# A block-sparse attention and gated Fourier convolution kernel: the forward transform of the last four pairs by two and then by three, the frequencies in another order, and a priority of its own for every operation

## The chip, the cores and the metric

The kernel runs on one core of a Trainium2 chip. The metric is the device time of one execution in microseconds (us). The kernel before was run three times: 232.38, 234.02 and 234.77 us, median 234.02 us.

## The reference

The inputs are q, k and v of shape (4 batches, 8 heads, 768 positions, 64 dimensions) and three matrices for the second half. For each head the 768 positions are cut into 12 blocks of 64. A query attends causally to its own block and to the three blocks whose mean key has the highest product with it:

```python
k_rep = k.reshape(B, H, n_blocks, block, D).mean(axis=3)
gate_scores = np.einsum('bhsd,bhnd->bhsn', q, k_rep)
...
top_idx = np.argsort(gate_scores, axis=-1)[..., -top_k:]
...
attn = softmax(q k^T / 8 where the mask allows) @ v
```

The attention output x, with heads side by side (768 x 512 for each batch), goes through a gated long convolution, which is circular over the 768 positions:

```python
proj = x @ w_proj                      # 512 -> 3 * 512: x1, x2, x3
X2 = np.fft.rfft(x2, n=S, axis=1)
H = np.fft.rfft(filter_fft, n=S, axis=0)[None, :, :]
x2_conv = np.fft.irfft(X2 * H, n=S, axis=1)
y = x1 * x2_conv * x3
return y @ w_out
```

The output is (4, 768, 512) in float32.

## The kernel before, in words

**Units of work.** Two heads make a pair; there are 16 pairs (index g), four for each batch. All data is in tiles of 128 partitions, matmuls run in float16 and accumulate in PSUM, which has 8 banks. While attention lasts, two pairs of banks hold scores, and four single banks serve everything else.

**Attention of a pair.** `prep(g)` loads k and q, transposes k on TensorE (L360), sums its blocks on VectorE (L363), copies it to `kt` on ScalarE (L373), does the same for q (L424, L427, L430), computes the gate (L483), finds the third largest value (L493 to L511) and puts the block mask beside the transposed q (L528, L535). Pairs from 9 on get the transposed q by transposing DMAs (L462, L466). `attn(g)` makes, for each of two heads, three pieces of scores (L558), the exponential on ScalarE (`ex`, L565), a causal cut of the diagonal on GpSimd (`sel`, L570), the product with v (`pv`, L588), and the division by the row sum on VectorE (L597, L601), which gives the tile `xn`. So there are 96 pieces of scores and 96 exponentials.

**The forward transform of a pair.** `xn` has 6 chunks of 128 positions. `eo` (L626, VectorE or GpSimd) adds and subtracts the two halves of the sequence: even frequencies need only the sum, odd ones only the difference, each of 3 chunks. `st1` then multiplies these chunks with a table `F` of cosines and sines: in part 0, three matmuls of 256 columns (L638) and six of 128 columns (L645), in part 1 three of 256 columns (L638). `XT` (L651, VectorE or ScalarE) evicts the result. A transposing DMA (L620) gives `xT`, the attention output with its 128 columns on partitions.

**The convolution of a batch.** `hyena(b)` needs all four pairs of its batch: `s2` projects the spectrum (L747), `t` multiplies it with the filter's spectrum `HA`, `HB`, `HA0` (L756, VectorE), `Y` combines the products (L766), `x13` computes the two gates x1 and x3 (L783), evicted as `x1` (L789) and `prod` (L792), `cv` goes back to positions (L810), `ce`, `sd`, `yT` (L819, L825, L831) finish the product, `op` is the output projection (L841), `osb` its eviction (L845) and a DMA (L848) stores it. The filter's spectrum is made once at the start: `hf` (L697, L702) and `ha` (L707, ScalarE).

**What sets the order.** Nothing in the kernel waits by hand. `build` lists all operations with what they read and write, a cost for each engine that may take them, and a due time `vt`. `plan` is a list scheduler: again and again it takes, on the engine that can start first, the ready operation of smallest due time, gives it buffers and, where several engines may run it, picks the one that would end it first (with a bias `d_<tag>` against VectorE). The instructions are then emitted in that order, each engine runs its own in order, and the compiler adds the semaphores. A due time is a formula in the pair's or batch's number with some 50 constants in `PAR`, and one offset `v_<tag>` shared by all operations of a kind:

```python
vt += self.par.get("v_" + tag, 0.0)
```

Until a planned time (`warm_until`) holes on TensorE are filled with matmuls whose results nobody reads (`filler`, L945, 128x256); there are 116. All loads and stores are issued by one queue, SyncE's. The semaphores of the DMAs are eight, used in turn, and a DMA waits for the one eight places ahead of it.

**What the change touches.** `PAR` and `Graph.add`; `e_phase`, `e_iota`, `e_nyq` (L178 to L198), which fill the row of frequencies `colv` that `F` is made from; the pool `eo` (three tiles of 128x384); `eo`, `st1` in `attn` (L555 to L656); `e_ha`, `e_h0` in `filt` (L706 to L721), and `e_t` in `hyena` (L753).

Of the kernel before, what the change touches and what calls it, by code (L numbers as in the profile page):

```python
# [16 lines left out]
P = 128  # L17
# [10 lines left out]
TR = ("T1", "T2", "xT")  # L28
QS = 128.0
# [15 lines left out]
for _pi, _segs in enumerate(PIECES):  # L45
    for (_col, _kc, _q0, _w) in _segs:
        for _c in range(_q0 // P, (_q0 + _w) // P):
# [4 lines left out]
    direct=2, tm=9, kin=16, p0=-2.69, p1=0.365, pvlag=-6.582, dlag=1.76, dlen=1.383, h0=4.856,  # L52
    hlen=3.36, f0=-1.155, f1=7.084, ld=-3.238, s2a=-2.037, s2b=1.216, x0=0.354, x1=1.108, c0=-1.101,
    c1=2.132, o0=1.271, ahead=46.953, delta=0.033, queue=5.995, w0=1.489, wl=1.839, wlag=-9.917, warm_until=32.306,
    tr0=-18.919, trl=6.39, fill0=0.877, v_yT=7.627, v_sd=-1.517, d_k2=6.956, v_trig=-4.154, v_ldq=1.131, v_max=-5.158,
    v_g=0.972, v_Y=0.635, v_k2=0.499, v_rec=-6.814, v_small=-3.021, v_gate=0.152, v_km=0.106, d_x1=3.233, d_shQ=2.566,
    v_xT=-0.742, v_prod=-3.06, v_ldv=0.502, d_yT=8.721, v_ks=0.515, v_osb=-10.289, v_ldk=0.513, v_kT=0.073, v_gT=-1.053,
    d_md=-0.495, d_trig=6.615, v_qT=0.164, v_mT=0.152, v_lt=-2.205, v_fe=7.674, d_eo=-0.025, v_md=-2.102, v_phase=2.124,
    v_shQ=5.115, v_ldf=0.27, d_Y=3.198, v_sel=-7.798, v_warm0=4.967, v_x1=-4.181, v_ldw=0.046, v_tab=0.848, v_va=5.426,
    v_iota=-3.776, d_XT=-0.933, v_qh=0.379, v_h0=4.716, v_eblk=9.913, v_id32=-1.815, v_st=2.29, v_nyq=-4.563, v_s2=-2.561,  # L60
    v_st1=-0.047, v_XT=-3.549, v_t=-1.696, v_ql=-0.667, v_hf=-3.271, d_g=2.878, d_ce=12.21, d_osb=6.098, d_fill=0.038,
    v_w=-6.92, v_ce=0.546, v_fill=7.615, v_op=0.842, v_pv=-3.144, d_w=0.456, v_nrm=4.319, v_ha=-6.505, v_id16=4.506,
    v_eo=3.749, v_x13=-0.318, d_fe=-2.864, v_cv=-2.842, v_sc=0.099, v_T2=-3.366, v_T1=-1.079, d_qh=1.789, v_pq=-5.732,
    d_pq=12.199, v_ex=0.491, v_nid=0.437, a0=0.0, o1=1.0, pen_dve=0.205, late=2.0,
)

POOLS = dict(kn=2, qn=3, vn=2, k2=1, qx=4, ks=2, km=3, m8=2, gs=2, nm=1,
             kt=4, qt=4, va=4, ex=8, rec=2, xn=2, eo=3, XT=7, xT=8, t=8, Y=1, x1=3,
# [15 lines left out]
class Op:  # L84
    __slots__ = ("i", "eng", "emit", "deps", "bufs", "alloc", "vt", "lock", "size", "tag",
                 "start", "done", "on", "pre", "nd", "succ", "ready", "quad")


class Graph:
    def __init__(self, par):  # L90
        self.ops, self.par = [], par

    def add(self, tag, vt, eng, emit, rd=(), wr=(), res=(), lock=False, size=0, quad=0):
        o = Op()
        vt += self.par.get("v_" + tag, 0.0)
        o.i, o.tag, o.vt, o.eng, o.emit, o.lock, o.size = len(self.ops), tag, vt, eng, emit, lock, size
        o.quad = quad
        deps = set()

        def norm(xs):  # L100
            return [x if isinstance(x, tuple) else (x, 0) for x in xs]

        bufs = []
        for b, p in norm(rd):
            deps.update(b.w.get(p, ()))
            b.r.setdefault(p, []).append(o)
            bufs.append(b)
        for b, p in norm(wr):
            deps.update(x for x in b.w.get(p, ()))
            deps.update(x for x in b.r.get(p, ()) if x is not o)  # L110
            b.w.setdefault(p, []).append(o)
            bufs.append(b)
        deps.discard(o)
        o.deps = list(deps)
        o.bufs = list({id(b): b for b in bufs}.values())
        for b in o.bufs:
            b.left += 1
        o.alloc = list({id(b): b for b in o.bufs + list(res)}.values())
        self.ops.append(o)
        return o  # L120
# [21 lines left out]
def build(par):  # L142
# [35 lines left out]
    def e_phase(E, nc, en):  # L178
        ph = E.colv[32:33, :]
        nc.vector.memset(E.rowv[32:33, :], 1.0)  # L180
        nc.vector.memset(E.rowv[64:65, :], TURNS)
        nc.vector.memset(ph, 192.0)
        for x_ in cviews(ph):
            nc.vector.memset(x_[:, :, 1, :], 0.0)
        nc.vector.memset(ph[:, P:P + 1], 192.0)
# [4 lines left out]
    def e_iota(E, nc, en):  # L190
        c3, c4 = cviews(E.colv[0:1, :])
        kw = dict(channel_multiplier=0, allow_small_or_imprecise_dtypes=True)
        nc.gpsimd.iota(c3, pattern=[[1, 2], [0, 2], [2, P]], base=0, **kw)
        nc.gpsimd.iota(c4, pattern=[[1, 2], [0, 2], [2, 64]], base=256, **kw)
        nc.gpsimd.iota(E.rowv[0:1, :], pattern=[[1, HS]], base=0, **kw)

    def e_nyq(E, nc, en):
        nc.vector.memset(E.colv[0:1, P:P + 1], 384.0)  # L198
# [78 lines left out]


    kn, qn, va = {}, {}, {}
    for g in range(NG):  # L280
        b, j = divmod(g, NP)
# [22 lines left out]

    fts = []
# [238 lines left out]
    def attn(g):  # L544
        b, j = divmod(g, NP)
        xn = Buf("xn")
        E_, O_ = Buf("eo"), Buf("eo")
# [75 lines left out]
        for dst, op, f in ((E_, ALU.add, 0.0), (O_, ALU.subtract, 0.1)):  # L623
            def e_eo(E, nc, en, dst=dst, op=op):
                x_ = E.sb(xn).rearrange("p c t d -> p c (t d)")
                (nc.vector if en == "DVE" else nc.gpsimd).tensor_tensor(  # L626
                    E.sb(dst), x_[:, 0:HC, :], x_[:, HC:NQ, :], op=op)
            add("eo", v(f), {"POOL": pol(0.87), "DVE": dve(HS, 2)}, e_eo, rd=xns, wr=[dst], lock=True)
        add("xT", v(.3), {"SP": (1.25, 0)}, e_xT, rd=xns, wr=[xT[g]], size=305)
        for p_ in range(2):  # L630
            st = psb()
            lo, hi = (0, 512) if p_ == 0 else (512, S)

            def e_st(E, nc, en, p_=p_, st=st):
                o = E.bk(st)
                ev, od = E.sb(E_), E.sb(O_)
                for c in range(HC):
                    nc.tensor.matmul(o[:, 0:256], lhsT=(od if p_ else ev)[:, c, :],  # L638
                                     rhs=E.F[:, c, HS * p_:HS * p_ + 256], start=(c == 0), stop=(c == HC - 1),
                                     skip_group_check=True)  # L640
                if p_ == 0:
                    o2 = o[:, 256:512].rearrange("p (k i n) -> p i k n", k=2, i=2)
                    for i, x_ in enumerate((ev, od)):
                        for c in range(HC):
                            nc.tensor.matmul(o2[:, i], lhsT=x_[:, c, :],  # L645
                                             rhs=E.F[:, c, HS * i + 256:HS * (i + 1)]
                                             .rearrange("p (k n) -> p k n", k=2),
                                             start=(c == 0), stop=(c == HC - 1), skip_group_check=True)

            def e_XT(E, nc, en, lo=lo, hi=hi, st=st):  # L650
                (nc.vector.tensor_copy if en == "DVE" else nc.scalar.copy)(  # L651
                    E.sb(XT[g])[:, lo:hi], E.bk(st)[:, 0:hi - lo])

            add("st1", v(.5 + .25 * p_), {"PE": pe_cost([c16(256)] * 3 + ([c16(128)] * 6 if p_ == 0 else []))},
                e_st, rd=[O_] + ([E_] if p_ == 0 else []) + Fall, wr=[st], res=[XT[g]])
            add("XT", v(.55 + .25 * p_), {"ACT": act(hi - lo), "DVE": dve(hi - lo)}, e_XT, rd=[st],  # L656
                wr=[(XT[g], p_)])


    def filt():  # L660
# [27 lines left out]
        for c in range(HC):  # L688
            for kind in range(2):
# [16 lines left out]
                def e_ha(E, nc, en, c=c, kind=kind, pa=pa):  # L706
                    nc.scalar.activation((E.HB if kind else E.HA)[:, c, :], E.bk(pa), AF.Copy, bias=0.0,  # L707
                                         scale=E.crow if c == 0 else 2.0 / S)
# [4 lines left out]
                add("ha", v(.45 + .1 * (2 * c + kind)), {"ACT": act(Dm)}, e_ha, rd=[pa, cb("small")],  # L713
                    wr=[(cb("HA" if kind == 0 else "HB"), c)])

        def e_h0(E, nc, en):
            nc.vector.tensor_copy(E.HA0, E.HA[:, 0, :])
            nc.vector.tensor_copy(E.HA0[0:1, :], E.HB[0:1, 0, :])
            nc.vector.memset(E.HB[0:1, 0, :], 0.0)

        add("h0", v(1.0), {"DVE": (1.1, 1.2)}, e_h0, rd=[(cb("HA"), 0)], wr=[(cb("HB"), 0), cb("HA0")], lock=True)  # L721


    def hyena(b):
# [11 lines left out]
        for c in range(HC):  # L736
            for kind in range(2):
# [15 lines left out]
                for i, dst in enumerate((ta, tb)):  # L753
                    def e_t(E, nc, en, c=c, kind=kind, i=i, dst=dst, xa=xa):
                        m = E.HB[:, c, :] if i else (E.HA0 if kind and c == 0 else E.HA[:, c, :])
                        nc.vector.tensor_mul(E.sb(dst), E.bk(xa), m)  # L756
                    add("t", v(f, "s2a", "s2b") + .02, {"DVE": dve(Dm)}, e_t,
                        rd=[xa, (cb("HA"), c), (cb("HB"), c), cb("HA0")], wr=[dst])
# [100 lines left out]
    for g in range(NG):  # L859
        prep(g)  # L860
    for g in range(NG):
        attn(g)
    filt()
    for b in range(B):
        hyena(b)
# [6 lines left out]
def plan(par):  # L872
# [210 lines left out]
    xn=([P, NQ, 2, D], FP16), eo=([P, HC, P], FP16), XT=([P, S], FP16), xT=([P, S], FP16),  # L1083
# [17 lines left out]
def kernel(  # L1101
# [22 lines left out]
    for name, shape, dt in (  # L1124
            ("id32", [P, P], FP32), ("id16", [P, P], FP16), ("eblk", [64, S], FP16), ("colv", [P, S], FP16),
            ("rowv", [P, HS], FP16), ("warm", [P, 256], FP16), ("tab", [1, 1], FP16), ("crow", [P, 1], FP32), ("nid", [P, P], FP16), ("F", [P, HC, S], FP16),
# [39 lines left out]
```

## Time and profile before

| | |
|---|---|
| median of three runs | 234.02 us |
| the profiled execution's own time | 235.11 us |
| its span, first to last instruction | 233.4 us |
| TensorE matmuls | 223.5 us busy (96%), 2189 |
| VectorE | 184.1 us busy (79%) |
| ScalarE | 176.2 us busy (75%) |
| GpSimd | 169.3 us busy (73%) |
| DMA, 16 engines | 40.91 MB, queue 1 holds 89.9% of the span |

The span is shorter than the execution's own time by 1.7 us, which lie before the first and after the last instruction. A busy TensorE is not a full one: matmuls are pipelined, and each is shown with the time in which its results drain. What a matmul takes from the engine is the distance to the start of the next one; in unbroken rows the timeline gives 216 ns for 512 columns, 162 ns for 384, 109 ns for 256 and for a float32 transpose, 55 ns for 128, about 32 ns for the 65 columns of `pv`. This document calls that distance a slot.

### The profile page before, as it was taken

How to read it: one execution, taken by the hardware profiler on the slowest of the kernel's cores; microseconds unless marked ns; L12 is line 12 of the kernel's file. 1: busy time of each engine (PE TensorE's matmuls, PEld its weight loads, DVE VectorE, ACT ScalarE, POOL GpSimd, SP SyncE). 2: the span in 40 equal slices, each digit the busy share in tenths (PEclk: the TensorE clock that was granted, in tenths of full speed). 3: DMA queues.
4: the chain of work that ended last, by engine and by line, in shares of the span. 5: the costliest groups of instructions: out<-in, count | busy, mean ns of one | idle time of the engine just before them, and what ended most of it. 6: DMA issues, size and time to landing. Idle time of an engine off the chain costs nothing.

```text
span 233.4 us, 6222 instructions
## 1 busy us (share of the span) xinstructions
PE 223.5 (96%) x2189; PEld 151.0 (65%) x2189; DVE 184.1 (79%) x615; ACT 176.2 (75%) x295; POOL 169.3 (73%) x309
## 2 busy tenths in 40 slices
PE   7999999989898899999999999999999999999993
PEld 5787786756666577667655677676557667545551
DVE  6999779779897989998899597887986856595730
ACT  2988999999996888889957787999376675405343
POOL 8156467778669799979789999774598666069760
PEclk9999999999999999999999999999999999999999
DMA  8999999898999999999999999959912310512015
GB/s 159 330 217 201 219 194 225 174 226 203 228 213 247 216 227 176 240 223 231 187 228 204 294 186 232 178 94 163 269 61 79 70 34 3 169 46 90 3 44 225
DMA packets 120223, 40.91 MB, mean 175 GB/s; under 512 B 114304, under 2 KB 114304, under 8 KB 120192
## 3 DMA queue, kind: packets, MB, share of 16 engines
q1 hardware_dynamic: 120192, 40.51, 89.9%
q8 instruction: 17, 0.28, 0.5%
q14 instruction: 14, 0.11, 0.2%
HBM read 24.64 MB, written 6.29 MB: 133 GB/s over the span
## 4 chain that ended last, share of the span: by engine, by line
PE 70%; ACT 10%; DMA 7%; DVE 6%; issue 3%; SPq 2%; POOL 1%; DVEq 0%; ACTq 0%
PE ps L783 15%; PE ps L558 9%; PE ps L841 9%; PE ps L747 7%; PE ps L588 7%; PE ps L810 6%; DMA t<-in_moe_w_proj_dram 4%; ACT ex L565 4%; PE ps L638 4%; DMA kn<-in_k_dram 3%; PE ps L360 3%; PE ps L945 3%; ACT kt L373 3%; PE ps L645 2%; DVE ks L363 1%
## 5 line engine op out<-in xcount | busy, mean ns | idle before, releaser
L565 ACT ACTIVATE ex<-ps 128x1024 f16<-128x1024 f32 (+1 forms) x96 | 86.4, 923 | 17.5 <-PE ps L558 16.5
L570 POOL TENSOR_SCALAR_AFFINE_SELECT ex<-ex 128x256 f16<-128x256 f16 x96 | 40.1, 425 | 23.0 <-ACT ex L565 21.1
L558 PE MATMUL ps<-qt,kt 76*128 76x512 f16 (+7 forms) x256 | 50.4, 305 | 0.6 <-ACT ex L565 0.4
L783 PE MATMUL ps<-xT,wp 128*128 128x384 f16 x256 | 49.8, 326 | 0.0
L766 POOL TENSOR_TENSOR Y<-t,t 128x512 f16<-128x512 f32 (+1 forms) x32 | 40.3, 1268 | 11.3 <-DVE t L756 10.2
L373 ACT CAST kt<-ps 64x384 f16<-64x384 f32 x64 | 30.1, 472 | 6.4 <-PE ps L360 4.2
L831 POOL TENSOR_TENSOR yT<-prod,sd 128x384 f16<-128x384 f32 x32 | 32.3, 1018 | 3.6 <-DVE sd L825 2.3
L783 PEld LDWEIGHTS <-wp 128*128 128x128 f16 x256 | 24.1, 97 | 14.5 <-issue 0.3
L558 PEld LDWEIGHTS <-kt 76*128 76x128 f16 (+1 forms) x256 | 23.4, 97 | 14.6 <-issue 0.8
L588 PE MATMUL ps<-va,ex 128*128 128x65 f16 x672 | 27.2, 193 | 1.6 <-POOL ex L570 1.1
L588 PEld LDWEIGHTS <-ex 128*128 128x128 f16 x672 | 25.5, 97 | 4.8 <-POOL ex L570 1.8
L789 ACT CAST x<-ps 128x384 f16<-128x384 f32 x32 | 15.3, 478 | 14.1 <-PE ps L783 12.5
L792 DVE TENSOR_TENSOR prod<-ps,x 128x384 f32<-128x384 f32 x32 | 17.6, 552 | 8.6 <-PE ps L783 8.1
L841 PE MATMUL ps<-wo,yT 128*128 128x512 f16 x96 | 23.3, 379 | 0.0
L747 PE MATMUL ps<-wp,XT 128*128 128x512 f16 x96 | 22.5, 379 | 0.1
L651 DVE CAST XT<-ps 128x256 f16<-128x256 f32 (+1 forms) x30 | 16.1, 544 | 5.6 <-PE ps L645 3.6
L845 ACT COPY osb<-ps 128x512 f32<-128x512 f32 x24 | 14.1, 589 | 8.3 <-PE ps L841 7.9
L945 PE MATMUL ps<-warm 128*128 128x256 f16 x116 | 18.3, 293 | 1.1 <-DVE warm L1133 1.1
L363 DVE TENSOR_REDUCE ks<-ps 128x6 f32<-128x384 f32 x32 | 17.3, 548 | 2.3 <-ACT kt L373 1.3
L810 PE MATMUL ps<-G,Y 128*128 128x384 f16 x96 | 19.0, 326 | 0.0
L601 DVE TENSOR_TENSOR xn<-ps,rec 128x384 f16<-128x384 f32 x32 | 17.6, 551 | 0.7
L825 DVE TENSOR_TENSOR sd<-ce,ps 128x384 f32<-128x384 f32 x32 | 16.3, 545 | 1.6 <-ACT ce L819 1.5
(107 smaller groups left out, 376.3 us busy)
## 6 DMA issues: line engine op xcount, KB each, us to landing
kn<-in_k_dram SPq DMA_DIRECT2D x32, 192.0 KB, 4.3
vn<-in_v_dram SPq DMA_DIRECT2D x16, 384.0 KB, 5.3
qn<-in_q_dram SPq DMA_DIRECT2D x32, 192.0 KB, 4.7
out_dram<-osb SPq DMA_DIRECT2D x24, 256.0 KB, 2.3
t<-in_moe_w_proj_dram SPq DMA_DIRECT2D x12, 256.0 KB, 4.5
t<-in_moe_filter_fft_dram SPq DMA_DIRECT2D x6, 256.0 KB, 4.6
qt<-qx SPq DMA_DIRECT2D x14, 96.0 KB, 3.9
t<-in_moe_w_out_dram SPq DMA_DIRECT2D x4, 256.0 KB, 3.9
```

The source lines that it names most:

```text
L373: (nc.scalar.copy if en == "ACT" else nc.vector.tensor_copy)(E.sb(Kt[g])[r, HC * hf:HC * (hf + 1), 1 - t, :], E.bk(kp)[r, 0:HS].rearrange( ...
L558: nc.tensor.matmul(o[:, col:col + w], lhsT=E.sb(Kt[g])[0:KR[t], kc, 1 - t, :], rhs=E.sb(Qt[g])[0:KR[t], q0 // P:(q0 + w) // P, 1 - t, :], ...
L565: nc.scalar.activation(E.sb(ex)[:, 0:w], E.sp(sp)[:, 0:w], AF.Exp, scale=ESC)
L570: nc.gpsimd.affine_select(out=dv, in_=dv, compare_op=ALU.is_ge, fill=0.0, base=0, pattern=[[0, 2], [1, P]], channel_multiplier=-1)
L588: nc.tensor.matmul(o[:, 65 * c:65 * c + 65], lhsT=E.sb(exs[pi])[:, col:col + P], rhs=E.sb(va[g])[:, t, kc, :], start=(kc == 0), stop=(kc = ...
L747: nc.tensor.matmul(E.bk(xa), lhsT=w, rhs=E.wp[:, j, Dm:2 * Dm], start=(j == 0), stop=(j == NP - 1))
L766: (nc.vector if en == "DVE" else nc.gpsimd).tensor_tensor(E.sb(Y)[ro, n_, :], E.sb(x)[ri, :], E.sb(y)[ri, :], op=op)
L783: nc.tensor.matmul(E.bk(xq)[:, 0:HS], lhsT=E.wp[:, d2, 2 * Dm * m + P * dc:2 * Dm * m + P * (dc + 1)], rhs=E.sb(xT[gs[d2]])[:, cs], start= ...
L810: nc.tensor.matmul(E.bk(cv)[:, 0:HS], lhsT=E.sb(Y)[:, 3 * p_ + n_, P * dc:P * (dc + 1)], rhs=E.G[:, 3 * p_ + n_, :], start=(n_ == 0), stop ...
L831: (nc.vector if en == "DVE" else nc.gpsimd).tensor_mul(E.sb(yT)[:, dc, cs], E.sb(prod)[:, cs], E.sb(sd)[:, cs])
L841: nc.tensor.matmul(E.bk(op_), lhsT=E.sb(yT)[:, d2, P * c:P * (c + 1)], rhs=E.wo[:, d2, :], start=(d2 == 0), stop=(d2 == NP - 1))
L945: nc.tensor.matmul(E.ps[:, 3584:3840], lhsT=E.warm[:, 0:P], rhs=E.warm[:, 0:256], start=True, stop=True)
```

## The change

There are three parts.

1. For pairs 12 to 15 (`r3=12`) the forward transform splits each half once more, by three. The three chunks of the sum are combined into: the sum of all three, the first minus half of the two others, and the difference of the two others, and so for the difference of the halves. Frequencies that are multiples of three need only the first of these, one matmul in place of three; the others need two, one with `F` and one with a new table `Dt`, which is made once from `F`. The additions are done by four VectorE instructions for a pair (`r3`), and the subtraction in `eo` becomes two instructions for these pairs.
2. So that the multiples of three lie together, the frequencies are put in another order in `colv`. The constant term and the highest frequency move from the first group of columns to the third, and with them the special cases in `ha`, `h0` and `t`.
3. The due time of each of the operations comes from a table `VT` (one number for every operation, by kind and number) in place of the formula and the shared offset. The constants in `PAR` have other values too. `ha` may now run on VectorE. `eo` is one tile for both halves (two buffers in place of three single ones), `es` is new.

```diff
+    r3=12, direct=2, tm=9, kin=16, p0=-2.685, p1=0.336, pvlag=-7.813, dlag=1.811, dlen=1.366,
...
+VT = {
+    "id32": (-20.541,),
...
+    "r3": (213.925, 161.149, 176.246, 161.579,),
...
-        vt += self.par.get("v_" + tag, 0.0)
+        n = self.count[tag] = self.count.get(tag, -1) + 1
+        vt = VT[tag][n] if VT else vt
...
-        nc.gpsimd.iota(c3, pattern=[[1, 2], [0, 2], [2, P]], base=0, **kw)
-        nc.gpsimd.iota(c4, pattern=[[1, 2], [0, 2], [2, 64]], base=256, **kw)
+        for g, step in ((0, 2), (1, 4)):
+            nc.gpsimd.iota(c3[:, g], pattern=[[0, 2], [6, 64], [step, 2]], base=2 - g, **kw)
+        nc.gpsimd.iota(c4, pattern=[[3, 2], [0, 2], [6, 64]], base=0, **kw)
...
+    def e_dt(E, nc, en):
+        eng = nc.vector if en == "DVE" else nc.gpsimd
+        for i, op in enumerate((ALU.subtract, ALU.add)):
+            f1, f2 = (E.F[:, t, HS * i:HS * i + 256] for t in (1, 2))
+            eng.tensor_tensor(E.Dt[:, i], f1, f2, op=op)
+            eng.tensor_scalar_mul(E.Dt[:, i], E.Dt[:, i], 0.5 - i)
...
+                if i and r3:
+                    eng.tensor_tensor(w[:, 0:3:2], x_[:, 0:HC:2], x_[:, HC:NQ:2], op=op)
+                    eng.tensor_tensor(w[:, 1], x_[:, HC + 1], x_[:, 1], op=op)
+                else:
+                    eng.tensor_tensor(w, x_[:, 0:HC, :], x_[:, HC:NQ, :], op=op)
...
+        if r3:
+            def e_r3(E, nc, en):
+                w, s_ = E.sb(W), E.sb(es)
+                nc.vector.tensor_tensor(s_, w[:, :, 1], w[:, :, 2], op=ALU.add)
+                nc.vector.tensor_tensor(w[:, :, 1], w[:, :, 1], w[:, :, 2], op=ALU.subtract)
+                nc.vector.tensor_tensor(w[:, :, 2], w[:, :, 0], s_, op=ALU.add)
+                nc.vector.scalar_tensor_tensor(out=w[:, :, 0], in0=s_, scalar=-0.5, in1=w[:, :, 0], op0=ALU.mult,
+                                               op1=ALU.add)
+            add("r3", v(.2), {"DVE": (1.1, 1.25)}, e_r3, wr=[(W, 0), (W, 1), es], lock=True)
...
+                if r3:
+                    terms = [(w[:, p_, 0], E.F[:, 0, HS * p_:HS * p_ + 256]), (w[:, p_, 1], E.Dt[:, p_])]
+                else:
+                    terms = [(w[:, p_, c], E.F[:, c, HS * p_:HS * p_ + 256]) for c in range(HC)]
+                for n_, (l_, f_) in enumerate(terms):
+                    nc.tensor.matmul(o[:, 0:256], lhsT=l_, rhs=f_, start=(n_ == 0), stop=(n_ == len(terms) - 1), **mm)
...
+                        terms = [(2, 0)] if r3 else [(c, c) for c in range(HC)]
...
-                add("ha", v(.45 + .1 * (2 * c + kind)), {"ACT": act(Dm)}, e_ha, rd=[pa, cb("small")],
+                add("ha", v(.45 + .1 * (2 * c + kind)), {"ACT": act(Dm), "DVE": dve(Dm)}, e_ha, rd=[pa, cb("small")],
...
-            nc.vector.tensor_copy(E.HA0, E.HA[:, 0, :])
+            nc.vector.tensor_copy(E.HA0, E.HA[:, 2, :])
```

The other operations are the same as before; their places in the orders of the engines, and for some the engine, are not.

## The prediction

> **What bounds the kernel now.** I read the page first, then TensorE's timeline, then a table by stages, then the waits in the stage that had holes, then the end. The table by stages (duration; busy us and instructions of PE, PEld, DVE, ACT, POOL; clock; DMA share; GB/s):
>
> ```profile
> core 0: us, PE busy (x) PEld busy (x) DVE busy (x) ACT busy (x) POOL busy (x), PEclk, DMA share, GB/s
> 0.00:34.00 34.00, 32.69 (x306) 24.85 (x307) 28.09 (x115) 27.61 (x55) 19.43 (x44) 1.00 1.09 221
> 34.00:82.00 48.00, 43.46 (x524) 30.81 (x521) 40.46 (x158) 43.45 (x70) 36.86 (x76) 1.00 1.15 216
> 82.00:230.00 148.00, 147.37 (x1367) 95.35 (x1365) 115.59 (x344) 104.77 (x171) 113.06 (x190) 1.00 0.80 151
> 230.00:233.40 3.40, 0.00 (x0) 0.00 (x0) 0.00 (x0) 0.37 (x1) 0.00 (x0) 1.00 0.45 173
> ```
>
> Three stages are to be seen. From 82 to 230 us TensorE is full and every other engine has room: DVE 78%, ACT 71%, POOL 76%. There a slot less on TensorE is a slot less of time. To 34 us the 116 filler matmuls stand between real ones (116 x 0.109 = 12.6 us). Between, PE has holes with ACT as the fullest engine:
>
> ```profile
> 40.00:60.00 20.00, 17.99 (x238) 13.19 (x237) 15.46 (x70) 19.35 (x31) 14.84 (x33) 1.00 1.04 210
> 60.00:80.00 20.00, 17.57 (x196) 11.85 (x194) 17.82 (x62) 16.85 (x29) 16.30 (x31) 1.00 1.25 211
> ```
>
> ACT is 97% busy from 40 to 60, 84% from 60 to 80, where DVE reaches 89%. Busy time hides part of the holes, since a matmul is shown longer than its slot. Going through the starts on TensorE's timeline and taking off each slot, I find 8.6 us of holes (those over 0.06 us) from 30 to 82, 1.2 before, 0.7 from 82 to 230. The waits of PE from 30 to 82 (total, times, longest) name the larger ones:
>
> ```profile
> PE ps L588 <- POOL ex L570: 1.1, 2, 0.7
> PE ps L360 <- DMA kn<-in_k_dram: 0.9, 2, 0.7
> PE ps L528 <- DVE ks L363: 0.6, 1, 0.6
> PE ps L558 <- ACT ex L565: 0.4, 1, 0.4
> ```
>
> By start distances the `pv` holes are 0.84, 0.29, 0.56 and 0.25 us (1.9 in all: 19 of 21 products wait for one causal cut), the `kn` holes 0.44 and 0.83 (1.3). The rest, 5.4 us, is over twenty holes of 0.1 to 0.5 us. The end, from the chain of waits (start, duration):
>
> ```profile
> 198.19 0.66 PE ps L588 x21
> 198.86 2.59 PE ps L841 x12
> ...
> 224.51 5.21 PE ps L841 x24
> 229.79 0.58 ACT osb L845
> ```
>
> Twelve projections of another batch cover what the last pair needs between its last `pv` and its `st1`.
>
> **What the Trainium skill says.** "TensorE: Matmul & The Clock Gate", section "Wait — 56ns, not 53.3ns?": a warm matmul starts N/2.4 GHz + 2.5 ns after the one before. The trace agrees: 109 ns for 256 columns, 55 for 128. "Perfetto Trace Analysis", section "Identifying the Most-Contended Engine": the most contended engine can change over a kernel, and matmul busy time is a poor measure; hence the count by stages and slots. "SBUF — State Buffer", section "Who interferes with whom": a VectorE instruction with two SBUF inputs and a GpSimd one that reads SBUF block each other. `eo` and `r3` are such; the trace fits, `eo` on DVE takes 347 ns at least, 420 in the median and 917 at most.
>
> **The change part by part.** The rows used:
>
> ```profile
> L638 PE MATMUL ps<-F,eo 128*128 128x256 f16 x96 | 15.7, 272 | 0.3
> L645 PE MATMUL ps<-F,eo 128*128 128x128 f16 x96 | 8.0, 219 | 0.0
> L626 DVE TENSOR_TENSOR eo<-xn 128x384 f16<-128x384 f16 x18 | 8.4, 482 | 0.1
> L626 POOL TENSOR_TENSOR eo<-xn 128x384 f16<-128x384 f16 x14 | 13.5, 963 | 0.0
> ```
>
> 1. *Matmuls of st1.* A pair has 6 x 0.109 + 6 x 0.055 = 0.98 us of slots; pairs 12 to 15 keep 4 x 0.109 + 2 x 0.055 = 0.55. Four times 0.44 is 1.75 us off TensorE, all after 150 us, where it is full: -1.75. The changed order has 118 fillers for 116: +0.22.
>
> 2. *VectorE work.* `r3` is four instructions of 256 columns, not in the trace; scaled from `eo` (384 columns), 0.23 us at the minimum and 0.32 at the mean, bounded by 0.6 if each is blocked once. I take 0.33: 1.3 us a pair. Its two subtractions replace one, +0.1. Four pairs: 5.6. `Dt` is four of 256, 1.2, once near the start. Counting both built orders: two `ha` come to DVE (2 x 0.68 = 1.4), seven `XT` evictions leave it (5 x 0.42 + 2 x 0.69 = -3.5), fills -0.9, `eo` of the first kind 18 to 19 (+0.5). Net +4.3 us at these prices, 0 to +9 at the bounds, on an engine that is idle 32 us in the full stage: nothing while they are hidden, and TensorE's work hides them. POOL gives five `eo` (-4.8) and takes fills, -3.8 in all. ACT: +3.1 for `XT`, -1.2 for `ha`: +1.9.
>
> 3. *The end.* Between the last `pv` and the last pair's `st1` the new order puts sixteen projections and 0.55 us of the pair before: 16 x 0.216 + 0.55 = 4.0 us of cover. The chain there is the divisions of both heads (0.2 + 2 x 0.55), `eo` (0.42 + 0.55), `r3` 1.3, some 0.4 of handing over: 4.0. Before it was 2.1 under 2.6. So it just fits: +0 to +1 us, I take +0.2. From the first `s2` of the last batch to its first `cv` there are 11.9 us of matmuls, before 10.8, and from the last `cv` to `op` 1.3 in both: nothing there. Behind `op` nothing is changed.
>
> 4. *Frequencies.* On POOL two instructions of 0.59 and 0.35 us become three of 0.35: +0.1 us, under VectorE's fills, which end at 6.4 us, 1.3 later than POOL's. Zero; 0.1 without cover. Special cases move with the columns.
>
> 5. *The places.* No operation is lost, so only holes can be gained or made: at most 8.6 + 1.2 + 0.7. Counting slots, the new order has 58.8 us of matmuls, fillers included, up to the 33rd piece of scores, the old one 57.6, with ACT's work up to the 33rd exponential 0.6 us less, and 1.6 less up to the 24th, the last of the first batch's attention. ACT sets the pace there, so about 1 to 1.8 us of holes should be filled by then. The second halves of k for pairs 7 and 8, whose loads end the two `kn` holes, stand four places earlier in SyncE's queue (places 57 and 65, before 61 and 69); at 1 us or more for a place both land before they are wanted: -1.3, or 0 if the queue is held by a DMA eight places before. They are queued behind fewer projections of weights, one of which comes later. `pv` of a head is split in the new order (15 and 6, 9 and 6 and 6), with transposes between, where it waited for a cut: I take 1.2 of the 1.9. Together I take 2.7 (bounds 0 and 8.6); the twenty small holes I leave.
>
> 6. *New waits.* DVE has 2 to 4 us more work ahead of the same steps in the stretch 60 to 110, where it is 90% full, and 5 more ahead of the last division. What comes late is then a PSUM bank, with `s2` or `x13` queued on it. I take +0.3; bounds 0 and 6.
>
> Sum: -1.75 + 0.22 + 0.2 - 2.7 + 0.3 = -3.7. The profiled execution has span 233.4 and time 235.1; so span 229.7, time 231.4. It lay 1.1 above the median of the runs, so from 234.0 I get **230.3**.
>
> **Rivals.**
> *A, most holes close.* For it: they are small, scattered and scheduling alone makes them. Against: the order of ACT up to 64 us has almost the same work as before and ACT has no room. With 7 of 8.6 filled: 234.0 - 1.5 - 7 + 0.2 = 225.7.
> *B, only the matmuls count.* The places gain nothing, since the holes come from ACT's pace and DMA arrivals: 234.0 - 1.5 + 0.2 = 232.7, within 1%. For it: ACT 97% full.
> *C, slower: DVE becomes the bound.* Place: from 160 us to the last `st1`, where DVE is busy 30.8 of 40 us and idle 9.2, and gets 5.0 more by the bare sum. With `r3` blocked by POOL at 0.6 each, 16 x 0.27 = 4.3 more, 9.3: all room is gone. Every further microsecond is TensorE's; in-order waits for banks start before. It decides once more than 3.9 us of it shows on TensorE (the gain without the late terms is 4.2); with 6.5 exposed the time is 234.0 - 4.2 + 6.5 = 236.3. Against it: the holes after 82 us were 0.7 with DVE at 78%.
> *D, the table does nothing*: excluded, since the built orders differ on all five queues.
>
> **How the numbers follow.** Forecast case 0.50 (own range 228.5 to 231.7), A 0.14, B 0.21, C 0.15. Faster by over 1% (below 231.7, about what a measurement of this kernel can tell): 0.48 of the forecast, 0.14 of A, 0.03 of B: 0.65. Slower by over 1% (above 236.4): 0.12, all from C. The rest, 0.23, is within 1%. The range leaves out half of A below and most of C above: 226.0 to 236.0.
>
> **What would show it.** Right: the two `kn` waits of PE gone; holes from 30 to 82 near 6 us; PE full from 80 to 226; `st1` of pairs 12 to 15 with 24 matmuls for 48; the last `st1` within 0.3 us of the projections before it. Wrong: DVE over 95% from 160 to 205 with PE waiting for `t`, `prod` or `r3` (C); holes as before (B) or under 3 us (A); `r3` instructions over 0.5 us; new waits at `T1`, `T2` or `kn`.

## The result, and the profile after

The changed kernel takes 241.12 us (median of four runs, 240.51 to 242.46), the kernel before 233.97 beside it: ratio 1.032, 95% interval 1.025 to 1.039. The forecast was 230.3 (226.0 to 236.0), so the sign was wrong. The profiled execution has span 240.7 and time 242.46; before it was 233.4 and 235.11.

The table by stages of the changed kernel, in the columns shown for the kernel before:

```profile
0.00:34.00 34.00, 29.77 (x227) 21.29 (x227) 27.20 (x94) 22.08 (x46) 19.89 (x38) 0.95 1.01 210
34.00:82.00 48.00, 43.36 (x552) 32.47 (x551) 42.70 (x162) 44.12 (x73) 34.99 (x74) 1.00 1.20 213
82.00:230.00 148.00, 144.40 (x1363) 93.50 (x1361) 126.39 (x380) 106.72 (x176) 109.89 (x192) 1.00 0.74 149
```

TensorE loses time in the first and the last row, which were full before, and gains nothing in the middle one. VectorE has 10.8 us more to do in the last row. The first row's clock is 0.95: TensorE ran at half its clock for 3.4 us, from 19.4 to 22.8 us.

The waits of PE from 30 to 82 us, and, in the second fence, after 82 us:

```profile
PE ps L687 <- ACT ex L694: 1.1, 2, 0.8
PE ps L656 <- ACT x L941: 1.1, 1, 1.1
PE ps L717 <- POOL ex L699: 0.8, 1, 0.8
```

```profile
PE ps L788 <- DVE xn L730: 1.5, 1, 1.5
PE ps L687 <- DVE qt L663: 0.8, 1, 0.8
PE ps L788 <- DVE eo L772: 0.7, 1, 0.7
```

(In the changed kernel L687 is scores, L694 the exponential, L699 the cut, L717 `pv`, L730 `xn`, L760 to L763 `eo`, L769 to L772 `r3`, L788 and L794 `st1`, L935 `x13`, L450 the weights' cast; the experiments' lines differ by a few.) The two `kn` waits are gone, as forecast. Others of the same size stand in their place, and `st1` now waits for VectorE.

I counted holes on TensorE's timeline as for the prediction (start distances less the slot, those over 0.06 us) in every kernel. "Clock" is the time lost at half clock. Spans, holes and clock are those of the profiled execution; times and ratios are of all runs, each against the kernel before on its chip (233.9 to 234.6 us).

| kernel | us | ratio (95%) | span | holes 0-34 | 34-110 | 110-150 | 150-206 | clock |
|---|---|---|---|---|---|---|---|---|
| before | 234.0 | | 233.4 | 1.3 | 9.2 | 0 | 0 | 0 |
| changed | 241.1 | 1.032 (1.025-1.039) | 240.7 | 4.4 | 8.9 | 0.8 | 2.9 | 1.7 |
| e1_iota | 240.6 | 1.026 (1.022-1.029) | 239.0 | 2.7 | 8.8 | 0.8 | 2.9 | 1.7 |
| e2_dt | 241.8 | 1.031 (1.026-1.035) | 240.7 | 3.0 | 12.4 | 0.8 | 2.9 | 0 |
| e3_both | 242.0 | 1.032 (1.028-1.035) | 240.6 | 1.7 | 12.4 | 0.8 | 2.9 | 1.7 |
| e4_alg | 248.9 | 1.063 (1.056-1.070) | 245.7 | 2.5 | 14.9 | 2.1 | 2.7 | 0 |
| e5_order_before_split | 240.9 | 1.032 (1.027-1.037) | 238.2 | 2.1 | 10.9 | 0 | 4.6 | 0 |
| e6_order_after_whole | 240.7 | 1.028 (1.022-1.033) | 239.6 | 1.2 | 12.1 | 0.8 | 0.2 | 1.7 |
| e7_weights | 241.6 | 1.034 (1.030-1.038) | 239.2 | 1.0 | 11.1 | 0.8 | 3.0 | 1.7 |
| e8_one_r3 | 239.3 | 1.024 (1.020-1.029) | 237.0 | 1.2 | 10.3 | 0.8 | 0.5 | 1.7 |
| e9_both_dt155 | 243.1 | 1.037 (1.030-1.043) | 242.5 | 1.0 | 12.8 | 0.8 | 4.2 | 1.7 |
| e10_split_dt155 | 237.2 | 1.014 (1.010-1.019) | 235.5 | 1.3 | 7.8 | 0 | 4.6 | 0 |
| e11_split_xt_act | 236.2 | 1.011 (1.006-1.015) | 235.9 | 2.1 | 8.2 | 1.0 | 3.9 | 0 |
| e12_before_start | 234.4 | 1.003 (1.001-1.005) | 233.8 | 3.2 | 7.7 | 0 | 0 | 0 |
| e13_casts_late | 241.4 | 1.031 (1.028-1.035) | 240.0 | 1.2 | 13.2 | 1.2 | 0.2 | 0 |
| e14_split_two | 234.4 | 1.003 (1.001-1.004) | 233.0 | 2.0 | 8.5 | 0 | 0.9 | 0 |
| e15_before_late_w | 243.4 | 1.039 (1.034-1.043) | 242.3 | 2.2 | 13.3 | 0 | 0 | 5.1 |
| e16_mended | 242.9 | 1.038 (1.034-1.042) | 241.2 | 1.2 | 12.6 | 1.2 | 4.2 | 0 |
| e17_after_half_w | 237.1 | 1.010 (1.005-1.016) | 236.5 | 0.8 | 10.8 | 0.8 | 0.2 | 0 |
| e18_before_half_w | 232.6 | 0.994 (0.991-0.998) | 231.4 | 1.1 | 7.0 | 0 | 0 | 0 |

For the changed kernel the sum closes: +3.1 of holes at the start, -0.3, +0.8, +2.9, 0.2 at the end, 1.7 of clock, -1.75 matmuls, +0.2 fillers: 6.9 of the 7.3 us that the span grew. Read like that, the start is the largest loss. The experiments do not bear this reading out. One profile is also a rough measure from 34 to 110 us: e3 and e8 have the same matmuls in the same order up to there, and yet 12.4 and 10.3 us of holes.

### The profile page after: what moved, and what is told of

It reads as the page before. It is cut to its first block, busy times and chain, and to the rows that moved or that the text cites. A ratio compares the mean times of both kernels' runs of the same rounds, so it can differ in the third digit from the quotient of the medians.

```text
span 240.7 us, 6196 instructions
## 1 busy us (share of the span) xinstructions
PE 224.5 (93%) x2167; PEld 150.3 (62%) x2167; DVE 198.3 (82%) x637; ACT 177.3 (74%) x300; POOL 168.6 (70%) x307
## 4 chain that ended last, share of the span: by engine, by line
PE 59%; DVE 16%; ACT 10%; POOL 7%; issue 4%; DMA 3%; SPq 0%; POOLq 0%; DVEq 0%; ACTq 0%
PE ps L935 14%; PE ps L687 9%; PE ps L993 8%; PE ps L899 8%; PE ps L717 6%; ACT ex L694 5%; PE ps L962 5%; ACT kt L501 3%; PE ps L788 3%; DMA t<-in_moe_w_proj_dram 3%; PE ps L488 2%; PE ps L794 1%; POOL colv L310 1%; DVE ks L491 1%; DVE prod L944 1%
## 5 line engine op out<-in xcount | busy, mean ns | idle before, releaser
L694 ACT ACTIVATE ex<-ps 128x1024 f16<-128x1024 f32 (+1 forms) x96 | 85.7, 922 | 11.3 <-PE ps L687 10.7
L699 POOL TENSOR_SCALAR_AFFINE_SELECT ex<-ex 128x256 f16<-128x256 f16 x96 | 41.2, 438 | 22.9 <-ACT ex L694 21.8
L687 PE MATMUL ps<-qt,kt 128*128 128x512 f16 (+7 forms) x256 | 49.9, 305 | 2.1 <-ACT ex L694 1.1
L918 POOL TENSOR_TENSOR Y<-t,t 128x512 f16<-128x512 f32 (+1 forms) x32 | 40.5, 1274 | 11.9 <-DVE t L908 10.6
L935 PE MATMUL ps<-xT,wp 128*128 128x384 f16 x256 | 48.0, 326 | 0.0
L983 POOL TENSOR_TENSOR yT<-prod,sd 128x384 f16<-128x384 f32 x32 | 31.6, 1004 | 6.2 <-DVE sd L977 4.4
L687 PEld LDWEIGHTS <-kt 76*128 76x128 f16 (+1 forms) x256 | 22.9, 97 | 17.8 <-issue 3.3
L935 PEld LDWEIGHTS <-wp 128*128 128x128 f16 x256 | 24.3, 97 | 15.0 <-issue 0.2
L717 PEld LDWEIGHTS <-ex 128*128 128x128 f16 x672 | 26.1, 98 | 5.2 <-POOL ex L699 2.1
L717 PE MATMUL ps<-va,ex 128*128 128x65 f16 x672 | 28.1, 193 | 1.3 <-POOL ex L699 1.1
L899 PE MATMUL ps<-wp,XT 128*128 128x512 f16 x96 | 23.6, 379 | 0.2 <-DVE t L908 0.2
L1101 PE MATMUL ps<-warm 128*128 128x256 f16 x118 | 19.3, 303 | 1.1 <-DVE warm L1289 1.1
L908 DVE TENSOR_TENSOR t<-ps,HB 128x512 f32<-128x512 f32 x24 | 15.9, 681 | 2.6 <-PE ps L899 1.9
L730 DVE TENSOR_TENSOR xn<-ps,rec 128x384 f16<-128x384 f32 x32 | 17.4, 552 | 0.6
```

The lines of the kernel that those rows point to most:

```text
L687: nc.tensor.matmul(o[:, col:col + w], lhsT=E.sb(Kt[g])[0:KR[t], kc, 1 - t, :], rhs=E.sb(Qt[g])[0:KR[t], q0 // P:(q0 + w) // P, 1 - t, :], ...
L694: nc.scalar.activation(E.sb(ex)[:, 0:w], E.sp(sp)[:, 0:w], AF.Exp, scale=ESC)
L699: nc.gpsimd.affine_select(out=dv, in_=dv, compare_op=ALU.is_ge, fill=0.0, base=0, pattern=[[0, 2], [1, P]], channel_multiplier=-1)
L717: nc.tensor.matmul(o[:, 65 * c:65 * c + 65], lhsT=E.sb(exs[pi])[:, col:col + P], rhs=E.sb(va[g])[:, t, kc, :], start=(kc == 0), stop=(kc = ...
L899: nc.tensor.matmul(E.bk(xa), lhsT=w, rhs=E.wp[:, j, Dm:2 * Dm], start=(j == 0), stop=(j == NP - 1))
L918: (nc.vector if en == "DVE" else nc.gpsimd).tensor_tensor(E.sb(Y)[ro, n_, :], E.sb(x)[ri, :], E.sb(y)[ri, :], op=op)
```

## The experiments

**The start.** Two iotas with an innermost loop of two take 1.52 us each (shown below), so the first sine matmul starts at 7.61 us in place of 6.49. `Dt` on VectorE stands ahead of the low half of q, and one of its multiplications takes 2.5 us. The first exponential comes at 28.1 us in place of 23.0.

e1 has another form of the iota with the same values, e2 emits `Dt` at a planned 100 us and leaves all else in its place, e3 does both, e9 both with 155 us:

```diff
-for g, step in ((0, 2), (1, 4)):
-    nc.gpsimd.iota(c3[:, g], pattern=[[0, 2], [6, 64], [step, 2]], base=2 - g, **kw)
+for j, sg in ((0, -1), (1, 1)):
+    nc.gpsimd.iota(c3[:, :, :, j::2], pattern=[[sg, 2], [0, 2], [6, 64]], base=2 + 2 * j, **kw)
...
+    if o.tag == "dt":
+        o.start = 100.0
```

> The changed kernel with the frequencies of the first two groups written by two other iota instructions, whose innermost loop has 64 steps in place of 2; same values, same place, nothing else moved. Theory S (start): the slow form costs 3.0 us of POOL where 0.9 stood before, the first sine matmul starts at 7.6 for 6.5 us, and what is lost at the start is never regained, because TensorE is full later. Then the first sine matmul is back at about 6.5, the wait of the gate for VectorE stays, and the time falls by about 1.1, from 241.1 to 240.0. Rival P (places): the loss is made by holes in the rest of the order and a late start is absorbed by them; then the time stays within 0.5 of 241.1 although the sine matmul is earlier.

> The changed kernel with the four instructions that make Dt emitted much later on VectorE (about the middle of its order, long before their first reader), everything else in its place. Theory S: Dt, one instruction of which took 2.5 us beside two GpSimd instructions, stood ahead of the low half of the first q, so the first gate came 1.9 us late, TensorE was quiet from 16.2 to 18.1 us and its clock was granted at half from 18.7 to 23 us, 1.7 us more. Then that wait and the slow clock are gone, the first exponential comes at about 24.5 for 28.1 us, and the time falls by 3.6 to 237.5. Rival P: the first exponential is earlier, but the time falls by less than 1. Rival K (clock only): the clock falls anyway, with 1.9 of the 3.6 gained.

> Both edits: the other iota and Dt late. Theory S: the first exponential within 0.5 us of the kernel before (23.0), the time down by 4.9 from 241.1 to 236.2, what is left over the kernel before being the late waits of st1 for VectorE (2.6 us at 193 and 198) less the 1.75 us of saved matmuls, and about 1 us of other holes. Rival P: 240 or more.

> e3_both with Dt at about 155 us instead of 100. In e2, e3, e7 and e8 the late Dt itself left a hole of 1 to 2.5 us at 105 us, which e1 (Dt at the start) has not, so that those runs priced the start together with a new wait. Theory S2 (the late start is real and was only paid back by this wait): the hole goes, 240.0 to 240.8, and PE's lag on the kernel before at 110 us falls from 3.6 to 2 us. Rival A (the stretch to 110 us is paced by the order of its transfers, whatever starts when): other holes open before 110 us, 241.5 to 242.3.

e1 is 0.5 us faster than the changed kernel by the medians and 1.1 us by the distance to the kernel before on its chip, but the intervals overlap, so it tells little. e2, e3 and e9 gained nothing against the changed kernel. In e3 the first exponential is back at 23.0 us, but the 49th stands at 110.9 us in both e2 and e3 (106.2 before), and the last output projection starts at 236.6 in the changed kernel, e2 and e3 alike. What the start gives back is lost before 110 us: 12.4 us of holes in place of 8.9. The late `Dt` has a part in that (1 to 2.5 us of a new hole at 105 us). In e9 this hole is gone, but others open before 110 us (12.8 us in all), and `Dt` makes one of 1.2 us where it now runs, from 162.9 to 164.8 us on VectorE, ahead of `xn`:

```profile
PE ps L993 <- DVE xn L730: 1.1, 1, 1.1
```

The counter-test, e12, puts only this start into the kernel before: the slow form of its iota, and `Dt`'s four instructions ahead of the same low half of q, into a tile that nothing reads:

```diff
-nc.gpsimd.iota(c3, pattern=[[1, 2], [0, 2], [2, P]], base=0, **kw)
+for g in range(2):
+    nc.gpsimd.iota(c3[:, g], pattern=[[0, 2], [4, 64], [2, 2]], base=g, **kw)
...
+return order[:at] + [o] + order[at:]
```

> The kernel before with only the changed kernel's start in it: the frequency table by iotas with an innermost loop of two (same values), and Dt's four VectorE instructions ahead of the same low half of q, unused. If a late start is paid in full in an order that was fitted to the early one: the first sine matmul 1.1 us and the gate 2 to 3 us later, 236.5 to 237.5. If the stretch to 110 us absorbs it: 234 to 234.8.

It costs 0.5 us. Its start is milder than that of the changed kernel: the first exponential comes at 25.15 us, 2.2 us late and not 5.2, and no half clock follows. TensorE lags behind the kernel before by 2.2 us at 34 us, by 1.3 at 50 and by 0.4 from 70 us on, so most of this delay is taken up. That all of a delay of 5 us would be taken up is not shown; what e3 shows is that taking it away from the changed kernel gains nothing.

**Split and order apart.** e4 keeps the split and goes back to due times from the formula. e5 emits the order of the kernel before and puts the split into it: `r3` behind the second `eo` on VectorE, `Dt` in `colv` when that is free. e6 emits the changed order with the old transform for all pairs, leaves out `r3` and `Dt`, and has e1's iota. e10 is e5 with `Dt` at 155 us.

In this order, e4, e5, e6, e10:

```diff
+VT = {}
...
-order = plan(PAR)
+order = split(plan(PAR))
...
+order = [o for o in order if o.tag not in ("dt", "r3")]
...
-T_DT = 100.0
+T_DT = 155.0
```

> The split by three for pairs 12 to 15 and the other order of frequencies, as in the changed kernel, with the slow iota and Dt early, but with the due times of the kernel before (formula, offsets and constants) in place of the table, and ha on ScalarE alone. Theory S: the start is late here too, by 1.1 for the iota, and by up to 3.6 more if Dt meets GpSimd's reads again; with 1.5 saved on st1: 233.6 without the meeting, 237.2 with it. Rival P (the table is what costs): 232.5, with a start as before. Rival D (r3 on VectorE costs the late waits under any order): 235 or more with a normal start.

> The order of the kernel before, every instruction in its old place, with the last four pairs split by three inside it (shorter matmuls, r3's four VectorE instructions behind the second eo, Dt at about 100 us, the frequencies in the new order by an iota whose innermost loop is long). Theory W (the planned places cost the time, the split itself does not): 234.6 less the matmuls' 1.75, so 232 to 233.5, and no late hole in front of st1 (L683/L691 or so) over 1 us. Theory D (the extra VectorE work before the last four pairs' first stage, slowed by GpSimd beside it, holds TensorE under any order): about 1.8 us per pair are late for st1, 236 to 239, with holes ahead of st1 between 180 and 205 us.

> The order of the changed kernel with the old whole transform for all pairs (no r3, no Dt, 12 matmuls where the split has fewer), and the fast iota. Theory W: the places alone cost it. From e3's 242.0, plus 1.75 for the matmuls, less the 2.9 us of late holes that r3 may own: 240 to 243, a loss of over 5 us against before with nothing of the split left in it. Theory D: without r3 the loss is gone, 236 or less.

> e5_order_before_split with Dt at about 155 us instead of 100: the order of the kernel before, with the split in it. The hole of 2.5 us at 105 us goes; if nothing else changes, 240.9 - 2.5 = 238.4, still with 4.5 us of holes between 176 and 206 us (theory D: r3's VectorE work). If the late holes close too, they came from the lag and not from r3: 234 or less.

e4 tells nothing of the parts: a planner fed with another list and the old due times makes a third order, worse than both. e5, e6 and e10 make the table that does tell:

| | whole transform | split by three |
|---|---|---|
| order before | 234.0 | 237.2 (e10) |
| changed order | 240.7 (e6) | 241.1 changed; 242.0 (e3); 243.1 (e9) |

Either part alone costs time, the order 6.8 us and the split 3.2, where `r3` stands as e10 puts it. The two do not add up: together they cost 7.1 us as built and 7.5 in e3, each against the kernel before on its chip (e9's 9.2 have the hole of the moved `Dt` in them). So the order is the main loss, and in the changed order the split adds less than a microsecond by these medians. e5's other 3.7 us were `Dt` at 100 us, 2.5 us on VectorE ahead of the copy to `qt`, for which TensorE then waited 2.3.

**Where the split loses.** From 150 to 206 us, holes: 0.2 in e6, 2.9 in the changed kernel, 4.6 in e10. VectorE in the changed kernel ahead of the late hole at 193.3 us:

```profile
190.78 0.34 DVE L769 TENSOR_TENSOR es<-eo 128x256 f16<-128x256 f16 x1
191.16 0.37 DVE L770 TENSOR_TENSOR eo<-eo 128x256 f16<-128x256 f16 x1
191.57 0.97 DVE L771 TENSOR_TENSOR eo<-eo,es 128x256 f16<-128x256 f16 x1
192.57 0.51 DVE L772 SCALAR_TENSOR_TENSOR eo<-es,eo 128x256 f16<-128x256 f16 x1
193.00 0.48 DVE L760 TENSOR_TENSOR eo<-xn 128x256 f16<-128x256 f16 x1
193.41 1.01 DVE L761 TENSOR_TENSOR eo<-xn 128x128 f16<-128x128 f16 x1
194.35 0.18 DVE L726 RECIPROCAL rec<-ps 128x6 f32<-128x6 f32 x1
194.56 0.56 DVE L730 TENSOR_TENSOR xn<-ps,rec 128x384 f16<-128x384 f32 x1
```

`r3` is done at 193.08, and yet its `st1` starts only at 195.18, right after `xn` ends at 195.12: by the wait above it needs what `xn` releases, a PSUM bank. `xn` stood behind `r3` and the next pair's divided subtraction, 3.6 us of VectorE work; in e6 only the undivided subtraction stands there, 0.36 us. L771 takes three times its shortest and L761 nearly five times; GpSimd ran `yT` from 191.36 to 192.39 and from 193.32 to 194.34. The Trainium skill, "SBUF — State Buffer", section "Who interferes with whom", has that a VectorE instruction with two SBUF inputs contends with a GpSimd instruction that reads SBUF. The trace agrees. e8 leaves out the first three of `r3`'s instructions (the fourth reads `eo` for `es`); e11 puts `XT` of the last four pairs on ScalarE; e14 splits only the last two pairs:

```diff
-nc.vector.tensor_tensor(s_, w[:, :, 1], w[:, :, 2], op=ALU.add)
-nc.vector.tensor_tensor(w[:, :, 1], w[:, :, 1], w[:, :, 2], op=ALU.subtract)
-nc.vector.tensor_tensor(w[:, :, 2], w[:, :, 0], s_, op=ALU.add)
...
+if o.tag == "XT" and o.group >= R3:
+    o.on = "ACT"
...
-R3 = 12
+R3 = 14
```

> e3_both with three of r3's four VectorE instructions left out, so the last four pairs' transform is not computed fully. Theory D: some 1.1 to 1.5 us per pair come off VectorE ahead of st1, the 2.9 us of holes between 180 and 205 us close for the most part, 239 to 240. Theory W: VectorE had room or the holes come from xn (late evictions) instead: 241.5 to 242.5.

> e10_split_dt155 with the evictions of the last four pairs' transform (XT) on ScalarE, which leaves VectorE's queue shorter by about as much (0.4 to 0.7 us each, 8 of them, 4.4 us) as r3 makes it longer (6 to 7 us). Theory D, in the form that VectorE's in-order queue is what st1 and x13 wait for: most of the late holes close, 235 to 237. Rival L, that it is the length of the chain of one pair (eo, r3, st1) and not the queue: the late holes stay, 238 or more.

> e10_split_dt155 (the order of the kernel before) with only the last two pairs split by three, not four. Theory D with the two places at 182 and 186 us, ahead of pairs 12 and 13, as the main price: these holes (2.1 us) and those at 173 us (0.9) go, the matmuls saved fall from 1.75 to 0.87 us: 237.2 - 3.0 + 0.9 = 235.1, and still not under the kernel before. If each pair pays the same: 235.5. If the loss came with Dt and the new frequencies instead: 237.

e8: ratio 1.024 for e3's 1.032 (5.3 us over the kernel before on its chip, e3 7.5), and late holes of 0.5 us in place of 2.9. So three of `r3`'s instructions in VectorE's queue make the late holes of the changed kernel. e11 is 1.0 us faster than e10, with intervals that overlap, and opened a hole of its own at 146 us; most of the late holes stay (3.9 us for 4.6), so it does not decide between the queue and the chain of one pair. e14 is 0.25% slower than the kernel before; its late holes are 0.9. PE waits in e10 and e14 after 150 us, the larger ones:

```profile
PE ps L807 <- DVE sd L849: 1.3, 1, 1.3
PE ps L653 <- DVE W L1137: 0.5, 1, 0.5
```

```profile
PE ps L653 <- DVE W L1137: 0.5, 1, 0.5
```

In e10 `x13` waits for a bank that `sd` frees: `r3` runs on VectorE from 185.69 to 187.14, `sd` behind it to 187.60, and `x13` starts at 187.65. Around the first two pairs VectorE has no room (8.2 of the 8.4 us from 180.6 to 189 are busy); for the last two pairs the split nearly pays for itself, no more.

**Where the order loses.** e6 differs from the kernel before in the order, with its choice of engines and its buffers for `eo`, and in the frequencies. The frequencies cost little: e14 has them too, with two pairs split, at 234.4 us. ScalarE's waits in it from 34 to 110 us, and the stages around its largest hole:

```profile
ACT wp L451 <- DMA t<-in_moe_w_proj_dram: 6.3, 4, 2.4
```

```profile
44.00:46.00 2.00, 1.66 (x24) 1.44 (x22) 2.00 (x6) 0.70 (x2) 1.27 (x2) 1.00 0.62 159
46.00:48.00 2.00, 0.80 (x11) 0.44 (x10) 1.76 (x4) 0.94 (x2) 0.79 (x4) 1.00 1.02 203
48.00:50.00 2.00, 1.34 (x15) 0.65 (x15) 0.59 (x2) 1.96 (x4) 0.11 (x1) 0.98 1.11 300
50.00:52.00 2.00, 2.00 (x19) 1.54 (x18) 1.48 (x16) 1.66 (x3) 1.36 (x4) 0.50 1.49 216
52.00:54.00 2.00, 2.00 (x23) 1.61 (x22) 1.59 (x7) 1.50 (x3) 1.72 (x4) 0.66 1.73 115
```

A cast of weights stands on ScalarE ahead of an exponential, waits 2.4 us for its transfer until 47.06, and TensorE has a hole of 2.0 us; then its clock is halved for 3.4 us (the third figure from the end of a line). Before, ScalarE waited 1.3 us for the weights of the projection, GpSimd 3.7; here 6.3 each. Four edits test it: e7 emits the loads of weights earlier (on e3), e13 and e16 the casts later (on e6 and e9), and e15 the loads later in the kernel before:

```diff
+if o.tag == "ldw":
+    o.start = max([min(o.start, max(o.start - 5.0, 36.0))] + [u.start + 0.01 for u in o.pre])
...
+if o.tag == "w":
+    o.start = max(o.start, min([o.start + 4.0] + [x.start - 1.0 for x in order if o in x.pre or o in x.deps]))
...
+if o.tag == "ldw":
+    o.start += 4.0
```

> e3_both (fast iota, late Dt) with the weight loads put up to 5 us earlier in SyncE's order. Theory W in the narrow form, that late weights and the casts behind them on GpSimd and ScalarE set the time at about 110 us: the hole at 106.8 us (1.46 us, gate behind w_out's cast) closes, PE's lead lost between 45 and 110 us (2.5 to 3.5 us) shrinks, time 239 to 240. Rival K, that the transfers' rate is the bound and what moves up pushes q, k or v back: the holes move to qT, kT or pv, time 241.5 to 243.

> e6_order_after_whole (the changed order, old transform) with the weights' casts up to 4 us later in their engines' queues, at least 1 us ahead of their first reader; every transfer keeps its place. Theory W2: in this order casts on ScalarE and GpSimd stand ahead of exponentials and selects while their weights are still under way (6.3 us of such waits on each engine), which makes the holes of 1.2 to 2.0 us at 46 and 66 us and the clock halved after them. Then the waits fall under 2 us, both holes close, and the time falls from 240.7 to 236 or 237.5. Rival K (whichever transfer is late, the stretch to 110 us is paced by all of them together): other holes open, 239.5 to 241.

> The kernel before with its weight loads 4 us later in SyncE's order and the casts where they were. Theory W2: the casts now wait for their weights and hold what is behind them, holes of 1 to 2 us open in front of pv and scores between 45 and 110 us: 236 to 239. Rival K or none: the other transfers come earlier by as much, 234 to 234.8.

> The changed kernel with the three places mended that the runs point to: the iota with a long innermost loop, Dt at 155 us, the casts up to 4 us later. Theory W2 with D: from e9's 243.1, less the 3 to 5 us of holes and clock: 238.5 to 240, the rest being r3's late holes (2.9 us) and places not found. Rival K: 241.5 to 243.

e15 shows that such waits can cost all of the loss and more: in the order before, weights loaded 4 us later cost 9.4 us. Its PE and ACT waits from 34 to 110 us:

```profile
PE ps L588 <- POOL ex L570: 4.2, 2, 2.3
PE ps L783 <- ACT x L789: 3.1, 1, 3.1
```

```profile
ACT wo L322 <- DMA t<-in_moe_w_out_dram: 3.9, 1, 3.9
```

But e13 and e16, in which ScalarE never waits for weights and GpSimd only once (1.7 us), gained nothing against e6 and e9, and e7 nothing that can be told (ratio 1.034, e3 1.032). In e7 v came late in turn (from the chain of waits), with a hole of 2.4 us and half the clock after it; in e13 PE waits for a gate and for `xn`:

```profile
68.85 6.37 DMA vn<-in_v_dram
75.34 0.91 POOL va L425
```

```profile
PE ps L936 <- DVE xn L731: 2.0, 1, 2.0
PE ps L553 <- DVE gs L625: 1.8, 1, 1.8
```

So the theory of the weights fell as the whole cause: each mended wait was replaced. Do the losses come through the transfers at all? e17 (on e6) and e18 (on the kernel before) load half of each weight and fill the other half of its columns with the first:

```diff
-nc.sync.dma_start(E.sb(f), src(E)[P * c:P * (c + 1)])
+nc.sync.dma_start(E.sb(f)[:, 0:256], src(E)[P * c:P * (c + 1), 0:256])
```

> e6_order_after_whole with half of each weight transfer (128 KB of 256), the other half of the weights' columns filled with the first: 2.1 MB less of the 16.5 MB that are moved between 34 and 110 us. Theory T (the changed order loses because its transfers come in another order while the queue is full): it gains most, to 235 or 236.5, and the difference to the kernel before with the same cut falls from 6.7 to 3 us or less. Theory Q (the loss is in the engines' in-order queues, where attention's steps wait for each other): 239.5 to 240.7, the difference stays 5 to 7 us.

> The kernel before with half of each weight transfer, as in e17. Theory T: the stretch before 110 us has 9.2 us of holes, some of which close: 231.5 to 233.5. Theory Q: 233.5 to 234.3.

The order before gains 1.4 us, the changed one 3.7, so the difference falls from 6.8 to 4.5 us, between what the two theories named. By the medians about a third of the order's loss comes through full transfers. The share is rough: e17's four runs spread over 3.1 us, and its profile is also without the half clock that cost e6 1.7 us. What makes the other 4.5 us is open: most of it lies in holes between 34 and 110 us, each with another releaser (`ex`, `qt`, `gs`, `xn`), and no single move closed them in sum.

## Why the prediction was wrong

*Step 5, the places (-2.7): failed, the main error.* The order alone costs +6.8 us (e6), and in the changed kernel the holes from 34 to 110 us are 8.9 us for 9.2: the 2.7 us did not come. The list of `kn` and `pv` holes was right, and the `kn` waits went; but I priced only the holes that would close. The bound of 0 to 8.6 rested on "no operation is lost, so only holes can be gained or made", and then took only gains; what a new order opens was left to step 6 (+0.3). Equal work up to the 33rd exponential, by sums of durations, said nothing of who waits for whom. From 34 to 110 us the order alone has 12.1 us of holes for 9.2, and loses 1.7 us at half clock. Which waits cause all of this stays open.

*Step 2, VectorE's work (nothing, hidden): failed.* In the order before, the split costs 3.2 us although it saves 1.75, so some 5 us are not hidden. Three errors of size: `Dt` took 3.9 us where I took 1.2, `r3` took 1.78 us a pair (304, 333, 482 and 659 ns) where I took 1.3, and I booked four subtractions off GpSimd without adding them to VectorE (L760 and L761, 0.94 us a pair). VectorE has 14.1 us more, not 4.3. The error of kind weighs more: idle time is no cover for an in-order queue. VectorE was busy 40.5 of 46 us from 160 to 206, 88%, and still held TensorE, since `xn` and `sd`, which free PSUM banks, stood behind `r3`. Rival C had this mechanism, with waits for banks, but put VectorE over 95% busy; it came at 88%. TensorE, which I had full from 80 to 226 us, has 6.1 us of holes there.

*Step 4, the frequencies (0): wrong in size and in its reason, nearly right in effect by luck.* 0.59 and 0.35 us became 1.52, 1.52 and 0.37. I took the price of one innermost loop for another, and VectorE's fills did not cover it: the first sine matmul starts 1.1 us late. In e12 a start with this iota and an early `Dt` cost only 0.5 us, since a later stretch took the delay up.

*Step 1 held:* `st1` of the four pairs has 24 matmuls for 48, and in e10 the span less its holes is 1.1 us shorter (forecast 1.75). *Step 3 held:* after 206 us there are 0.2 us of holes (forecast 0.2). *Step 6* had the right kind (+0.3, up to 6) and far too small a value.

## What to carry to other kernels

Price a new order by what stands ahead of each releaser, not by the holes that it is meant to close; and build both halves of a mixed change (old order with the new work, new order with the old work) before believing a story. A budget of holes that closes to 0.4 us still named the wrong cause: the start's 4.8 us of holes and clock could be taken away (e3) with nothing gained, and in e12 a stretch further on took up all but 0.4 of a delay of 2.2 us. Work put on a partly idle engine is free only where no bank or tile that the bound engine waits for is released behind it.

## What the hardware showed that I had not expected

The iota's time follows its innermost loop, not its size (changed kernel, e3, before):

```profile
L310 POOL IOTA colv<- 1x256 f16 x2 | 3.0, 1522 | 0.0
```

```profile
L310 POOL IOTA colv<- 1x256 f16 x2 | 0.7, 406 | 0.0
```

```profile
L193 POOL IOTA colv<- 1x512 f16 x1 | 0.6, 587 | 0.0
```

256 elements with an innermost loop of 2 take 1.52 us, with one of 64 and a stride of 2 in the output 0.41; 512 with one of 128 take 0.59.

A multiplication of 128x256 float16 by a constant on VectorE (`Dt`, L400) took 2.50 us from 14.61 to 17.11, with GpSimd's copies of `qt` and its cut of `va` beside it, and 0.23 us alone. The Trainium skill, "SBUF — State Buffer", section "Who interferes with whom", has that such an instruction can use the port pair that VectorE shares with GpSimd, and that then one of the two blocks fully. The trace fits: the slow one ends within 0.1 us of the cut of `va`.

Half clock came for 3.4 us at a time (1.68 us lost) in seven of the twenty profiles of the table, and three times as much in e15. The Trainium skill, "TensorE: Matmul & The Clock Gate", section "What's actually happening", gives half clock after an idle window of about 3.4 us. The length agrees: it is 3.41 us. But no such window was idle here: in e6 TensorE was busy 1.56 us of the 3.41 before half clock began, in the changed kernel 1.49. Nor is a long hole enough: e10 has 1.5 us at 186 us and e17 2.1 us at 46 us, at full clock.

The records of the clock show more. In each of the twenty profiles all its changes stand whole multiples of 3.413 us apart (in e15 half clock begins at 53.55, 108.16 and 241.28 us: 16 and 39 times 3.413). Cut the time at full clock into stretches of this grid: each in which TensorE was busy less than 1.5 us was followed by half clock, none with more than 1.95, and between the two both happened. So a hole can count by how it falls on the grid. In e6 the one of 2.0 us lies within one stretch (46.52 to 49.93 us), and with the half clock behind it cost nearly twice its length; in e17 the one of 2.1 us crosses into the next stretch at 46.79 us, and the emptier of the two has 1.64 us of work.
